# Phase changes of a fused transformer training kernel: PE transposes for two FFN groups, an earlier weight load, later tail loads

## Chip, cores and metric

One core of one Trainium2 chip. The time is device microseconds (us) of a whole execution. The kernel before took 3183.05 us in the median of its first three runs (3180.48 to 3196.14), all "fast" (within 1.5% of the fastest run of the same kernel). In the views PE is TensorE with its matmuls, DVE is VectorE, ACT ScalarE, POOL GpSimd, and SP (SPq: its queue) is SyncE, which here issues loads, DMA transposes and some stores. PE's results stand in banks of PSUM until DVE or ACT copies them out ("evacuation").

## The reference

A forward pass and its gradients. The reference is one `jax.vjp` over this function (2048 tokens, model width 448, 16 heads of 256, 8 memory rows, 64 segments of 32 tokens, FFN width 1792, all bf16):

```python
for s in range(n_seg):                       # recurrent: each segment needs the memory of the last
    xs = x[:, s*seg_len:(s+1)*seg_len, :]
    h = concatenate([mem, xs], axis=1)       # 8 + 32 rows
    q, k, v = h @ Wq, h @ Wk, h @ Wv         # 16 heads of 256
    p = softmax(where(mask, q k^T * scale, -1e9))
    o = (p v) @ Wo
    mem = o[:, :M, :]; outs.append(o[:, M:, :])
# ...
h  = x + A_ref(layernorm(x), mem0, Wq, Wk, Wv, Wo)
h2 = h + (silu(ln(h) @ w_gate) * (ln(h) @ w_up)) @ w_down
# outputs: h2 and the gradients of x, mem0, Wq, Wk, Wv, Wo, w_gate, w_up, w_down
```

## The kernel before

It has four phases: the forward chain over 64 segments; the FFN, forward and backward, in 8 groups of 256 tokens; the backward chain over the segments from 63 to 0; and the tail, which multiplies the weight gradients out of tensors that the other phases stored in DRAM. `W(o, ...)`, `A(o, ...)` and `B(o, ...)` are views at byte offset `o` (in KB per partition) of three fixed SBUF arenas. Different phases use the same bytes, and the dependence between two users of a byte becomes a wait. Names like X_q, M_v, DHb, VG or T0k are such tensors in DRAM. A scheduler orders each engine's instructions; `issue_after(x)` places an instruction behind `x` on the same engine.

The FFN's inputs are turned by PE for group 0 only, by DMA transposes on SP for the others; its products z, u and g are turned by DMA transposes and stored (in the last group u and g by PE):

```python
for n, gi in enumerate(groups):
    if n > 0:
        load_in(n, gi)                       # h and dout of the group, on SP
    for tt in range(G):
        # ... hn = (h - mean) * rstd  on DVE
        for src, dst in ((hn_t, hnT), (dout_t, doT)):
            if n == 0:
                # 4 PE transposes into PSUM, one evacuation
            else:
                nc.sync.dma_start_transpose(out=dst[:, :, tt*P:(tt+1)*P], in_=src)
    # ...
    proj(Wg_sb, hnT, gate)                   # ACT: sg = sigmoid(ps); DVE: g = ps * sg
    proj(Wu_sb, hnT, up)
    proj(WdT_sb, doT, dzf)
    # ... z, u, g -> Zt, DGP, DU:
    #     nc.sync.dma_start_transpose(out=stg, in_=...); nc.gpsimd.dma_start(out=dst, in_=stg)
```

The backward chain's weights go to the bytes that the FFN's weights leave; each segment writes its results to one of five buffers `blk_b`:

```python
blk_b = [A(8 * i, 32, P) for i in range(5)]
# ... loads on SP, in the program's order: segment 63's Q and K, To, v of 63, Tv, Tk, Tq
# (in the trace Tq stands ahead of Tk)
blk = {nm: blk_b[(3 * tb + i) % 5] for i, nm in enumerate("vkq")}
# ... in the last segment (s == 0), after its first products:
k.tl.grads(0)                                # tail loads of DHb, on SP
k.tl.outs(0, 3, 0, 6)                        # tail loads of X_o, on SP
```

The tail's first product reads those loads. Pieces of M_v are fetched by POOL into `ld_b = [A(33.5, ...), B(0, ...)]`, packed by DVE and ACT, and turned by PE for a later product.

Of the kernel before, what the change touches and what calls it, by code (L numbers as in the profile page):

```python
# [15 lines left out]
P = 128  # L16
# [249 lines left out]
class _FFNLoads:  # L266

    def __init__(self, k):
        W, D, F, KC, FC, G = k.W, k.D, k.F, k.KC, k.FC, 2
        self.k = k  # L270
        self.Wg_sb, self.Wu_sb = W(0, KC, F), W(14, KC, F)
        self.WdT_sb, self.Wd_sb = W(64, KC, F), W(78, FC, D)
        self.WgT_sb, self.WuT_sb = W(96, FC, D), W(108.25, FC, D)
        self.h_b = [W(32 + 0.875 * i, D) for i in range(4)]
        self.dout_b = [W(39.5 + i, k.DP) for i in range(4)]

# [18 lines left out]
    def at(self, place):  # L295
        k, sync = self.k, self.k.nc.sync
        if place == 0:
            self.rows(self.Wg_sb, k.aps["B_w_gate"])
            self.rows(self.Wu_sb, k.aps["B_w_up"])
        elif place == 1:  # L300
            self.load_in(0, 0)
        elif place == 2:
            self.turned_rows(self.WdT_sb, k.dr["Td"])
            sync.dma_start(out=self.Wd_sb, in_=k.aps["B_w_down"].rearrange("(c p) d -> p c d", p=P))
        else:
            sync.dma_start(out=self.WgT_sb, in_=k.dr["Tg"])
            return sync.dma_start(out=self.WuT_sb, in_=k.dr["Tu"])


class _TailLoads:  # L310

    def __init__(self, k):
        W, A, NT, NB = k.W, k.A, k.NT, k.NB
        self.k = k
        self.slots = [W(17.5 + 4 * i, 2048) for i in range(3)] + [A(25.5 + 4 * i, 2048) for i in range(2)] \
            + [A(48 + 4 * i, 2048) for i in range(3)] + [W(60, 2048), W(92, 2048)] + [W(96 + 4 * i, 2048) for i in range(7)] \
            + [W(32 + 4 * i, 2048) for i in range(7)] + [W(64 + 4 * i, 2048) for i in range(7)] + [A(17.5 + 4 * i, 2048) for i in range(2)]
        self.n = 0
        self.order = list(range(NT, NB)) + list(range(NT - 1, -1, -1))
        self.DCt = W(0, NB, k.D)  # L320
        self.x = {}

    def ring(self):
        self.n += 1
        return self.slots[(self.n - 1) % len(self.slots)]

    def grads(self, part):
        k, D, S, NT, M, SEG = self.k, self.k.D, self.k.S, self.k.NT, self.k.M, self.k.SEG
        sync, DHb = k.nc.sync, k.dr["DHb"]
        dcx = DHb[0:S, 0:D].rearrange("(t r i) d -> r i t d", r=4, i=SEG)  # L330
        dcm = DHb[S:, 0:D].rearrange("(t r m) d -> r m t d", r=4, m=M)
        dc8 = DHb[0:S, 0:D].rearrange("(g s i) d -> g s i d", s=16, i=SEG)
        if part == 0:
            for g in range(k.NB - NT):
                sync.dma_start(out=self.DCt[:, NT + g], in_=dc8[g, :, 0:M])
        for r in range(4):
            if part == 0:
                sync.dma_start(out=self.DCt[32 * r:32 * r + 24, :NT], in_=dcx[r, M:SEG])
                sync.dma_start(out=self.DCt[32 * r + 24:32 * r + 32, 4:NT], in_=dcm[r, :, 4:NT])
            else:  # L340
                sync.dma_start(out=self.DCt[32 * r + 24:32 * r + 32, 0:4], in_=dcm[r, :, 0:4])

    def outs(self, i0, i1, c0, c1):
        for t in self.order[i0:i1]:
            if t not in self.x:
                self.x[t] = self.ring()
            self.k.nc.sync.dma_start(out=self.x[t][:, c0 * P:c1 * P], in_=self.k.dr["X_o"][t][:, c0 * P:c1 * P])

# [438 lines left out]
def ffn_phase(k: _K, back):  # L787
# [14 lines left out]
    h_b, dout_b, load_in = fl.h_b, fl.dout_b, fl.load_in  # L802
    hn_b = [W(35.5 + i, DP) for i in range(4)]
    hnT_b = [W(28 + 2 * i, KC, G * P) for i in range(2)]
    doT_b = [W(43.5 + 2 * i, KC, G * P) for i in range(2)]
    t1 = W(47.5, G, FC, P)
    z_b = [A(56, G, FC, P), A(21, G, FC, P)]
# [24 lines left out]

    def tmajor_pe(src, t, tt, dst, i):
        stg = A(3.5 * i, F)
        for c0 in (0, 8):
            n = min(8, FC - c0)
            pt = k.ps1()[:].bitcast(BF16)
            for c in range(n):
                nc.tensor.transpose(pt[:, c * P:(c + 1) * P], src[:, tt, c0 + c, :], k.ident[:, :])
            k.evac(stg[:, c0 * P:(c0 + n) * P], pt[:, 0:n * P])  # L840
        nc.gpsimd.dma_start(out=dst[t * P:(t + 1) * P, :], in_=stg)

    def tmajor(src, t, tt, dst, z_last=False):
        stg = tstg_b[1 + tt] if z_last else tstg_b[rot[0] % 3]
        rot[0] += 1
        nc.sync.dma_start_transpose(out=stg, in_=src[:, tt].rearrange("p f n -> p (f n)"))
        nc.gpsimd.dma_start(out=dst[t * P:(t + 1) * P, :], in_=stg.rearrange("p f n -> p (f n)"))
# [19 lines left out]
    for n, gi in enumerate(list(range(last - 1)) + [last, last - 1]):  # L867
        hnT, doT = hnT_b[n % 2], doT_b[n % 2]
        if n > 0:
            load_in(n, gi)  # L870
        if n == last - 3:
            rstd(NT - 4, NT)
        if n == last:
            back()
        for tt in range(G):
# [7 lines left out]
            for src, dst in ((hn_t, hnT), (dout_t, doT)):  # L883
                if n == 0:
                    pt = k.ps1()[:].bitcast(BF16)
# [3 lines left out]
                else:  # L889
                    nc.sync.dma_start_transpose(out=dst[:, :, tt * P:(tt + 1) * P], in_=src)  # L890
            nc.gpsimd.dma_start(out=dr["HN"][rows, :], in_=hn_t[:, 0:D])
        e = n % 2
        g, z, dz, u, sg = g_b[e], z_b[e], dz_b[e], u_b[e], sg_b[e]
# [25 lines left out]
        for tt in range(G):  # L919
            t = G * gi + tt  # L920
            rows = slice(t * P, (t + 1) * P)
            tmajor(z, t, tt, dr["Zt"], n == last)
            pf = k.fx1()
# [3 lines left out]
            nc.vector.tensor_tensor(out=o_t, in0=pf[:, 0:D], in1=h_b[2 * e + tt], op=ALU.add)  # L927
            nc.gpsimd.dma_start(out=OUT0[rows, :], in_=o_t)
        for tt in range(G):
            nc.vector.tensor_tensor(out=u[:, tt], in0=dz[:, tt], in1=u[:, tt], op=ALU.mult)  # L930
            nc.vector.tensor_tensor(out=u[:, tt], in0=u[:, tt], in1=sg[:, tt], op=ALU.mult)
            nc.vector.tensor_tensor(out=g[:, tt], in0=dz[:, tt], in1=g[:, tt], op=ALU.mult)
        if n == last:
            back()
        for tt in range(G):
            t = G * gi + tt
# [17 lines left out]
        if n == last:  # L954
            for tt in range(G):
                t = G * gi + tt
                tmajor_pe(u, t, tt, dr["DGP"], 2 * tt)
                tmajor_pe(g, t, tt, dr["DU"], 2 * tt + 1)


def backward_chain(k: _K):
# [38 lines left out]
    def load_seg(s):  # L1000
        if s < NSEG - 1:
            load_v(s)
        for w, (nm, T_sb) in enumerate((("q", Q_sb), ("k", K_sb))):
            t1 = dr["T1"][s, :, w].rearrange("(g x i) n -> g i x n", g=2, x=2)
            t0 = dr["T0" + nm][s // 8].rearrange("(x s i) (g n) -> s g i x n", x=2, s=8, g=2)
            for g in range(2):
                for src, i0, i1 in ((t1[g], M, L), (t0[s % 8, g], 0, M)):
                    nc.sync.dma_start(out=T_sb[64 * g + i0:64 * g + i1].rearrange("p (x c) n -> p x (c n)", x=2), in_=src)
        P_sb = Pb[s % 2]
# [19 lines left out]
    prep_tile(NT - 1)  # L1029
    load_seg(NSEG - 1)  # L1030
    yield
    nc.sync.dma_start(out=WoT_sb[:, 0:3, :], in_=dr["To"][:, 0:3, :])
    nc.sync.dma_start(out=WoT_sb[0:64, 3, :], in_=dr["To"][0:64, 3, :])
    nc.gpsimd.memset(WoT_sb[64:P, 3, :], 0.0)
    yield
    v_in = load_v(NSEG - 1)
    with tc.issue_after(v_in.ins):
        nc.sync.dma_start(out=WvT_sb, in_=dr["Tv"])
    yield
    nc.sync.dma_start(out=WkT_sb, in_=dr["Tk"])  # L1040
    nc.sync.dma_start(out=WqT_sb, in_=dr["Tq"])
# [17 lines left out]
    for s in range(NSEG - 1, -1, -1):  # L1059
# [4 lines left out]
        lo = {nm: lo_b[nm][tb % len(lo_b[nm])] for nm in "kqv"}  # L1064
        blk = {nm: blk_b[(3 * tb + i) % 5] for i, nm in enumerate("vkq")}
        P_sb = Pb[s % 2]
# [5 lines left out]
        with k.prio.crit():  # L1072
# [26 lines left out]
            if s == 0:  # L1099
                k.tl.grads(0)  # L1100
                k.tl.outs(0, 3, 0, 6)
            pD3 = pD[:, 0:8 * L].rearrange("p (h n) -> p h n", n=L)
# [10 lines left out]
            def heads(nm, lhs, rhs):  # L1113
# [8 lines left out]
                if s == 0:  # L1122
                    k.tl.outs(*{"v": (3, 8), "k": (8, 9), "q": (9, 10)}[nm], 0, 6)

# [20 lines left out]
            rows_in("q", WqT_sb, 0, MC)  # L1145
            nc.vector.tensor_copy(out=om[:, 0:224], in_=pH[:, 0:224])
            nc.scalar.copy(out=om[:, 224:D], in_=pH[:, 224:D])
# [69 lines left out]
def tail_phase(k: _K):  # L1217
# [39 lines left out]
    def load_m(nm, hf):  # L1257
        todo = []
        for g in range(NG):
# [4 lines left out]
            def pack(ld=ld_b[g % 2], pk=pk_b[g % 2]):  # L1264
                nc.vector.tensor_copy(out=pk[:, 0:8], in_=ld[:, :, 0:8, :].rearrange("p s c m -> p c s m"))
                nc.scalar.copy(out=pk[:, 8:16], in_=ld[:, :, 8:16, :].rearrange("p s c m -> p c s m"))
# [9 lines left out]

    tl.outs(10, NB, 0, 6)
    tl.grads(1)
    tl.outs(0, NB, 6, 11)
    tl.outs(0, NB, 11, 16)  # L1280
    xo = tl.x
    nc.gpsimd.dma_start(out=HC, in_=dr["HC"].rearrange("(t p) d -> p t d", p=P)[:, :, 0:D])

# [39 lines left out]
    for hf in range(2):  # L1323
        xt = xo if hf == 0 else load_x("o", 1)
        j0 = 0
        for n in (6, 5, 5):
# [3 lines left out]
            rows_by_d(lambda b, i, j0=j0: xt[b][:, (j0 + i) * P:(j0 + i + 1) * P], lambda b: DCt[:, b, :], order, n, st)  # L1330
            j0 += n

    HN = W(0, NB, D)
# [99 lines left out]
```

## Time and profile before

| phase | from (us) | to (us) | length |
|---|---|---|---|
| forward chain | 0 | 1061.4 | 1061.4 |
| FFN, 8 groups | 1061.4 | 1409.0 | 347.6 |
| first backward segment (63) | 1409.0 | 1458.4 | 49.5 |
| segments 62 to 1 | 1458.4 | 2482.8 | 1024.3 |
| last segment (0), until the first tail matmul | 2482.8 | 2528.6 | 45.9 |
| tail | 2528.6 | 3198.7 | 670.1 |

These stretches come from PE's timeline: each begins with the first matmul of a known line (L855, L1079 of segments 63, 62 and 0, L1315). In a timeline a line has start, duration, engine, source line, operation, `out<-in`, form, count, and in brackets the idle time before it with what ended it. The prediction shows the lines of before.

### The profile page before, as it was taken

To read this page: it belongs to the slowest core of one execution; us is meant where nothing else is said; L and a number is where in the kernel's file an instruction comes from. 1 tells how busy PE (TensorE), PEld (TensorE's weight loads), DVE (VectorE), ACT (ScalarE), POOL (GpSimd) and SP (SyncE) were. 2 spreads that over 40 slices of the span, in tenths; PEclk is the share of its full clock that TensorE was granted. 3 is DMA by queue.
4 is the path that set the end of the run, shared out by engine and by line. 5 is a ranking of instruction groups with operands and counts; after the bars stand their busy time and mean duration, and the time that the engine had idled before them with its cause. 6 is when DMAs were issued, how large, how long until landed. Compare 5 with 4: busy or idle time off the path is not lost.

```text
span 3198.7 us, 107919 instructions
## 1 busy us (share of the span) xinstructions
PE 2917.2 (91%) x47442; PEld 1759.8 (55%) x47442; DVE 1367.3 (43%) x3433; ACT 1058.5 (33%) x2501; POOL 666.7 (21%) x1540
## 2 busy tenths in 40 slices
PE   6899999999998679968999999999999699999998
PEld 3555555555544456656666666666666454444443
DVE  4555455455455457654444544454444201111110
ACT  2444344344344233323333333333333101111110
POOL 2222222222222221121111211112111111111111
PEclk9999999999999889988999999999999899999999
DMA  6677666666756988894445555445445898969942
GB/s 235 169 170 176 172 168 176 172 170 167 196 156 164 280 194 194 197 309 107 126 138 137 143 138 140 126 131 155 132 138 145 262 266 223 199 181 194 197 142 66
DMA packets 763753, 556.21 MB, mean 174 GB/s; under 512 B 627732, under 2 KB 662404, under 8 KB 760852
## 3 DMA queue, kind: packets, MB, share of 16 engines
q1 hardware_dynamic: 708116, 373.96, 49.2%
q0 software_dynamic: 55168, 175.36, 16.3%
q8 instruction: 372, 6.09, 0.8%
q14 instruction: 97, 0.79, 0.1%
HBM read 167.32 MB, written 234.23 MB: 126 GB/s over the span
## 4 chain that ended last, share of the span: by engine, by line
PE 72%; DVE 9%; issue 8%; DMA 6%; ACT 3%; POOL 1%; SPq 1%; ACTq 0%; POOLq 0%; DVEq 0%
PE psf L1294 8%; PE po L1128 7%; PE psf L1079 6%; PE psf L526 5%; PE psf L637 5%; PE po L682 4%; PE psf L1056 4%; PE psf L1315 4%; PE fx L1192 3%; PE fx L945 2%; PE psf L855 2%; PE fx L455 2%; DVE arA L75 2%; PE psf L540 2%; PE fx L1299 2%
## 5 line engine op out<-in xcount | busy, mean ns | idle before, releaser
L75 DVE CAST arA<-psf 128x256 bf16<-128x256 f32 (+3 forms) x933 | 426.6, 479 | 826.1 <-PE psf L1294 258.9
L76 ACT CAST arA<-psf 128x96 bf16<-128x96 f32 (+5 forms) x915 | 352.4, 409 | 1084.7 <-PE psf L1294 256.5
L1128 PE MATMUL po<-arW,arA 128*32 128x448 bf16 x6144 | 351.2, 359 | 21.7 <-DVE arA L75 20.8
L1294 PE MATMUL psf<-arW,arA 128*128 128x512 bf16 x1000 | 252.0, 379 | 0.0
L1079 PEld LDWEIGHTS <-arW 128*128 128x128 bf16 x8192 | 213.9, 96 | 30.3 <-issue 30.3
L1079 PE MATMUL psf<-arA,arW 128*128 128x40 bf16 x8192 | 218.0, 180 | 11.1 <-issue 5.8
L1128 PEld LDWEIGHTS <-arA 128*32 128x32 bf16 x6144 | 152.7, 97 | 135.9 <-DVE arA L75 22.0
L1294 PEld LDWEIGHTS <-arA 128*128 128x128 bf16 x1440 | 135.9, 98 | 164.8 <-issue 13.7
L637 PE MATMUL psf<-arW,arA 128*64 128x512 bf16 x1536 | 219.7, 387 | 0.0
L855 PE MATMUL psf<-arW 128*128 128x256 bf16 x1344 | 155.4, 277 | 57.9 <-DMA arW<-arW 45.6
L526 PE MATMUL psf<-arW,arA 128*32 128x512 bf16 x3072 | 194.7, 386 | 12.5 <-DVE arA L724 12.5
L855 PEld LDWEIGHTS <-arW 128*128 128x128 bf16 x1344 | 133.1, 99 | 82.3 <-DMA arW<-arW 43.2
L76 ACT CAST arB<-psf 128x64 bf16<-128x64 f32 (+3 forms) x384 | 121.9, 318 | 146.1 <-PE psf L530 106.0
L682 PE MATMUL po<-arW,arA 128*32 128x256 bf16 (+1 forms) x4096 | 144.5, 267 | 10.8 <-DVE arA L75 7.5
L1056 PEld LDWEIGHTS <-arW 128*128 128x128 bf16 x2048 | 87.7, 100 | 90.4 <-issue 59.8
L1056 PE MATMUL psf<-arB,arW 128*128 128x80 bf16 x2048 | 98.2, 202 | 42.0 <-DMA arW<-T0k 23.1
L1089 ACT COPY arA<-psf 128x1024 bf16<-128x1024 bf16 x128 | 123.4, 1015 | 2.6 <-PE psf L1088 1.2
L526 PEld LDWEIGHTS <-arA 128*32 128x32 bf16 x3072 | 70.6, 97 | 90.8 <-DVE arA L724 18.1
L682 PEld LDWEIGHTS <-arA 128*32 128x32 bf16 x4096 | 95.8, 98 | 33.5 <-DVE arA L75 10.5
L455 PE MATMUL fx<-arA,arW 128*128 128x64 bf16 (+1 forms) x2048 | 84.2, 195 | 32.2 <-ACT arB L76 19.4
L76 ACT COPY arA<-psf 128x512 bf16<-128x512 bf16 (+2 forms) x136 | 79.0, 582 | 94.2 <-DVE arA L75 91.4
L455 PEld LDWEIGHTS <-arW 128*128 128x128 bf16 (+1 forms) x2048 | 70.6, 98 | 54.5 <-issue 32.7
(281 smaller groups left out, 4581.1 us busy)
## 6 DMA issues: line engine op xcount, KB each, us to landing
arW<-T SPq DMA_DIRECT2D x256, 128.0 KB
X_o<-arA SPq DMA_DIRECT2D x33, 512.0 KB
T<-arA SPq DMA_DIRECT2D x64, 256.0 KB
X_v<-arA POOLq DMA_DIRECT2D x32, 512.0 KB, 6.2
X_k<-arA POOLq DMA_DIRECT2D x32, 512.0 KB, 3.7
X_q<-arA POOLq DMA_DIRECT2D x32, 512.0 KB, 3.3
out_dram<-arA POOLq DMA_DIRECT2D x90, 128.0 KB, 4.0
VG<-arA SPq DMA_DIRECT2D x64, 160.0 KB
```

The costliest lines, as they stand in the source:

```text
L75: return nc.vector.tensor_copy(out=out, in_=in_)
L76: return nc.scalar.copy(out=out, in_=in_)
L455: nc.tensor.matmul(banks[w][:, i * 64:(i + 1) * 64], lhsT=lhsT, rhs=xr[lo:hi, kc, :], start=(kc == 0 and i == 0), stop=(kc == KC - 1), ski ...
L526: nc.tensor.matmul(banks[w][32 * q:32 * q + 32, :], lhsT=hT_roll[:, kc, sl, M:L], rhs=(Wq_sb, Wk_sb)[w][:, kc, col(q, b)], start=(kc == 0) ...
L637: nc.tensor.matmul(pV[b][64 * g:64 * g + 64, 0:512], lhsT=hT_flat[:, kc, sl * L:sl * L + 64], rhs=Wv_sb[:, kc, n * 512:(n + 1) * 512], sta ...
L682: nc.tensor.matmul(pO[32 * q:32 * q + 32, 0:w], lhsT=xblk[:, j, r * SEG:(r + 1) * SEG], rhs=Wo_sb[:, cj(j), 256 * dh:256 * dh + w], start= ...
L855: nc.tensor.matmul(ps[:, f2 * 256:(f2 + 1) * 256], lhsT=Wt[:, kc, c * P:(c + 1) * P], rhs=xT[:, kc, :], start=(kc == 0), stop=(kc == KC - 1))
L1056: nc.tensor.matmul(ps[b][:, i * 2 * L:(i + 1) * 2 * L], lhsT=lhs[:, at, :], rhs=rhs_bd[:, cl // 2, :, :].rearrange("p g n -> p (g n)"), st ...
L1079: nc.tensor.matmul(pss[b][:, jj * L:(jj + 1) * L], lhsT=WoT_sb[:, kc, c * P:(c + 1) * P], rhs=do_roll[:, kc, sl, :], start=(kc == 0), stop ...
L1128: nc.tensor.matmul(pH[32 * (j % 4):32 * (j % 4) + 32, 0:D], lhsT=blk[nm][:, j, r * SEG:(r + 1) * SEG], rhs=WT[:, cj(j), :], start=(nm == " ...
L1294: nc.tensor.matmul(pa[2 * kc + g][:, 0:w], lhsT=lhs_of(b)[:, kc * P:(kc + 1) * P], rhs=rhs_of(b, g), start=(b == 0), stop=(b == nblk - 1), ...
L1315: nc.tensor.matmul(pa[i][:, 0:D], lhsT=lhs_of(b, i), rhs=rhs_of(b), start=(bi == 0), stop=(bi == len(nblk) - 1))
```

## The change

The intent is to close the three gaps where phases meet: turn group 1 by PE too and load its inputs ahead; turn the last group's z by PE, load three quarters of Wk turned (Tk) during that group, and move `blk` by two buffers; let the last segment's K load go ahead of the tail loads. The core of the diff:

```diff
-        self.h_b = [W(32 + 0.875 * i, D) for i in range(4)]
-        self.dout_b = [W(39.5 + i, k.DP) for i in range(4)]
+        self.h_b = [W(o + 0.875 * i, D) for o in (37.75, 32) for i in range(2)]
+        self.hn_b = [W(o + i, k.DP) for o in (39.5, 33.75) for i in range(2)]
+        self.dout_b = [W(o + i, k.DP) for o in (41.5, 35.75) for i in range(2)]
@@ loads ahead of the FFN
             self.load_in(0, 0)
+            self.load_in(1, 1)
@@ FFN
-        if n > 0:
+        if n > 1:
             load_in(n, gi)
-                if n == 0:
+                if n < 2:
                     pt = k.ps1()[:].bitcast(BF16)     # PE transposes
@@ last group
-            tmajor(z, t, tt, dr["Zt"], n == last)
+            if n < last:
+                tmajor(z, t, tt, dr["Zt"])
@@ last group, after its products u and g
+                tmajor_pe(z, G * gi + tt, tt, dr["Zt"], (W(120.5, F), B(5, F))[tt])
@@ backward chain, weights
+    nc.sync.dma_start(out=WkT_sb[:, 8:MC], in_=dr["Tk"][:, 8:MC])
     yield
     # To ... Tv ... v of segment 63
-    nc.sync.dma_start(out=WkT_sb, in_=dr["Tk"])
+    nc.sync.dma_start(out=WkT_sb[:, 0:8], in_=dr["Tk"][:, 0:8])
     nc.sync.dma_start(out=WqT_sb, in_=dr["Tq"])
-        blk = {nm: blk_b[(3 * tb + i) % 5] for i, nm in enumerate("vkq")}
+        blk = {nm: blk_b[(3 * tb + i + 2) % 5] for i, nm in enumerate("vkq")}
@@ tail loads (all of grads(0) and outs)
+                with k.tc.issue_after(k.last_load.ins):
                     sync.dma_start(out=self.DCt[:, NT + g], in_=dc8[g, :, 0:M])
-                k.tl.outs(0, 3, 0, 6)
+                k.tl.outs(0, 7, 0, 6)
```

Cut: other slots for the tail's X_o tiles, the load of HC moved behind half of the first tail products, an `issue_after` for the first pack, and a `t1` and a `doT` buffer of their own for the last group.

More of the change, by code (lines that the diff above doesn't have):

```diff
@@ L314, in __init__ @@
         self.k = k
-        self.slots = [W(17.5 + 4 * i, 2048) for i in range(3)] + [A(25.5 + 4 * i, 2048) for i in range(2)] \
-            + [A(48 + 4 * i, 2048) for i in range(3)] + [W(60, 2048), W(92, 2048)] + [W(96 + 4 * i, 2048) for i in range(7)] \
-            + [W(32 + 4 * i, 2048) for i in range(7)] + [W(64 + 4 * i, 2048) for i in range(7)] + [A(17.5 + 4 * i, 2048) for i in range(2)]
+        self.first = [W(17.5 + 4 * i, 2048) for i in range(3)] + [A(4 * i, 2048) for i in range(4)]
+        self.slots = [A(48 + 4 * i, 2048) for i in range(3)] + [W(60, 2048), W(92, 2048)] + [W(96 + 4 * i, 2048) for i in range(7)] \
+            + [W(32 + 4 * i, 2048) for i in range(7)] + [W(64 + 4 * i, 2048) for i in range(7)] + [A(17.5 + 4 * i, 2048) for i in range(4)] + self.first[0:3]
         self.n = 0
@@ L323, in ring @@
     def ring(self):
+        if self.first:
+            return self.first.pop(0)
         self.n += 1
@@ L334, in grads @@
             for g in range(k.NB - NT):
-                sync.dma_start(out=self.DCt[:, NT + g], in_=dc8[g, :, 0:M])
+                with k.tc.issue_after(k.last_load.ins):
+                    sync.dma_start(out=self.DCt[:, NT + g], in_=dc8[g, :, 0:M])
         for r in range(4):
             if part == 0:
-                sync.dma_start(out=self.DCt[32 * r:32 * r + 24, :NT], in_=dcx[r, M:SEG])
-                sync.dma_start(out=self.DCt[32 * r + 24:32 * r + 32, 4:NT], in_=dcm[r, :, 4:NT])
+                with k.tc.issue_after(k.last_load.ins):
+                    sync.dma_start(out=self.DCt[32 * r:32 * r + 24, :NT], in_=dcx[r, M:SEG])
+                    sync.dma_start(out=self.DCt[32 * r + 24:32 * r + 32, 4:NT], in_=dcm[r, :, 4:NT])
             else:
@@ L346, in outs @@
                 self.x[t] = self.ring()
-            self.k.nc.sync.dma_start(out=self.x[t][:, c0 * P:c1 * P], in_=self.k.dr["X_o"][t][:, c0 * P:c1 * P])
+            with self.k.tc.issue_after(self.k.last_load.ins):
+                self.k.nc.sync.dma_start(out=self.x[t][:, c0 * P:c1 * P], in_=self.k.dr["X_o"][t][:, c0 * P:c1 * P])
 def forward_chain(k: _K):
@@ L802, in ffn_phase @@
     h_b, dout_b, load_in = fl.h_b, fl.dout_b, fl.load_in
-    hn_b = [W(35.5 + i, DP) for i in range(4)]
+    hn_b = fl.hn_b
     hnT_b = [W(28 + 2 * i, KC, G * P) for i in range(2)]
     doT_b = [W(43.5 + 2 * i, KC, G * P) for i in range(2)]
-    t1 = W(47.5, G, FC, P)
+    t1_b = [W(47.5, G, FC, P), A(14, G, FC, P)]
+    doT_last = A(0, KC, G * P)
     z_b = [A(56, G, FC, P), A(21, G, FC, P)]
@@ L831, in ffn_phase, with tmajor_pe @@
     rot = [0]
-    def tmajor_pe(src, t, tt, dst, i):
-        stg = A(3.5 * i, F)
+    def tmajor_pe(src, t, tt, dst, stg):
         for c0 in (0, 8):
@@ L841, in tmajor_pe, with tmajor @@
         nc.gpsimd.dma_start(out=dst[t * P:(t + 1) * P, :], in_=stg)
-    def tmajor(src, t, tt, dst, z_last=False):
-        stg = tstg_b[1 + tt] if z_last else tstg_b[rot[0] % 3]
+    def tmajor(src, t, tt, dst):
+        stg = tstg_b[rot[0] % 3]
         rot[0] += 1
@@ L867, in ffn_phase @@
     for n, gi in enumerate(list(range(last - 1)) + [last, last - 1]):
-        hnT, doT = hnT_b[n % 2], doT_b[n % 2]
-        if n > 0:
+        hnT, doT = hnT_b[n % 2], doT_b[n % 2] if n < last else doT_last
+        t1 = t1_b[n == last]
+        if n > 1:
             load_in(n, gi)
@@ L872, in ffn_phase @@
             rstd(NT - 4, NT)
-        if n == last:
-            back()
         for tt in range(G):
@@ L891, in ffn_phase @@
             nc.gpsimd.dma_start(out=dr["HN"][rows, :], in_=hn_t[:, 0:D])
+        if n == last:
+            back()
         e = n % 2
@@ L928, in ffn_phase @@
             nc.gpsimd.dma_start(out=OUT0[rows, :], in_=o_t)
+        if n == last:
+            back()
         for tt in range(G):
@@ L934, in ffn_phase @@
             back()
+            for tt in range(G):
+                tmajor_pe(z, G * gi + tt, tt, dr["Zt"], (W(120.5, F), B(5, F))[tt])
         for tt in range(G):
@@ L956, in ffn_phase @@
                 t = G * gi + tt
-                tmajor_pe(u, t, tt, dr["DGP"], 2 * tt)
-                tmajor_pe(g, t, tt, dr["DU"], 2 * tt + 1)
+                tmajor_pe(u, t, tt, dr["DGP"], A(7 * tt, F))
+                tmajor_pe(g, t, tt, dr["DU"], A(7 * tt + 3.5, F))
 def backward_chain(k: _K):
@@ L1007, in load_seg @@
                 for src, i0, i1 in ((t1[g], M, L), (t0[s % 8, g], 0, M)):
-                    nc.sync.dma_start(out=T_sb[64 * g + i0:64 * g + i1].rearrange("p (x c) n -> p x (c n)", x=2), in_=src)
+                    k.last_load = nc.sync.dma_start(out=T_sb[64 * g + i0:64 * g + i1].rearrange("p (x c) n -> p x (c n)", x=2), in_=src)
         P_sb = Pb[s % 2]
@@ L1035, in backward_chain @@
     yield
-    v_in = load_v(NSEG - 1)
-    with tc.issue_after(v_in.ins):
-        nc.sync.dma_start(out=WvT_sb, in_=dr["Tv"])
+    nc.sync.dma_start(out=WvT_sb, in_=dr["Tv"])
     yield
-    nc.sync.dma_start(out=WkT_sb, in_=dr["Tk"])
+    load_v(NSEG - 1)
+    yield
+    nc.sync.dma_start(out=WkT_sb[:, 0:8], in_=dr["Tk"][:, 0:8])
     nc.sync.dma_start(out=WqT_sb, in_=dr["Tq"])
@@ L1122, in heads @@
                 if s == 0:
-                    k.tl.outs(*{"v": (3, 8), "k": (8, 9), "q": (9, 10)}[nm], 0, 6)
+                    k.tl.outs(*{"v": (7, 10), "k": (10, 11), "q": (11, 12)}[nm], 0, 6)
             def rows_in(nm, WT, j0, j1):
@@ L1145, in backward_chain @@
             rows_in("q", WqT_sb, 0, MC)
-            nc.vector.tensor_copy(out=om[:, 0:224], in_=pH[:, 0:224])
+            k.last_om = nc.vector.tensor_copy(out=om[:, 0:224], in_=pH[:, 0:224])
             nc.scalar.copy(out=om[:, 224:D], in_=pH[:, 224:D])
@@ L1264, in pack @@
             def pack(ld=ld_b[g % 2], pk=pk_b[g % 2]):
-                nc.vector.tensor_copy(out=pk[:, 0:8], in_=ld[:, :, 0:8, :].rearrange("p s c m -> p c s m"))
+                with tc.issue_after(k.last_om.ins):
+                    nc.vector.tensor_copy(out=pk[:, 0:8], in_=ld[:, :, 0:8, :].rearrange("p s c m -> p c s m"))
                 nc.scalar.copy(out=pk[:, 8:16], in_=ld[:, :, 8:16, :].rearrange("p s c m -> p c s m"))
@@ L1275, in load_m @@
         return todo
-    tl.outs(10, NB, 0, 6)
+    tl.outs(12, NB, 0, 6)
     tl.grads(1)
@@ L1281, in tail_phase @@
     xo = tl.x
-    nc.gpsimd.dma_start(out=HC, in_=dr["HC"].rearrange("(t p) d -> p t d", p=P)[:, :, 0:D])
     def d_by_e(lhs_of, rhs_of, nblk, widths, store, at=None):
@@ L1331, in tail_phase @@
             j0 += n
+        if hf == 0:
+            nc.gpsimd.dma_start(out=HC, in_=dr["HC"].rearrange("(t p) d -> p t d", p=P)[:, :, 0:D])
     HN = W(0, NB, D)
```

## The prediction

> **What bounds the kernel now.** I read the page first, then the PE waits, then the chain of waits around each phase boundary, last the timelines of the queues that feed PE there.
>
> The page says that PE is busy for 91% of the span, and its row of 40 slices (80 us each) falls to 6 or 7 around 1040 to 1200, 1360 to 1440 and 2480 to 2560, where phases change (the first slice is the start).
>
> ```profile
> PE 2917.2 (91%) x47442; PEld 1759.8 (55%) x47442; DVE 1367.3 (43%) x3433; ACT 1058.5 (33%) x2501; POOL 666.7 (21%) x1540
> PE   6899999999998679968999999999999699999998
> ```
>
> So time can only be won where PE stands idle. The view of PE's waits between 1040 and 2560 us (engine, line, what it waited for, total, times, longest) holds few long ones:
>
> ```profile
> PE psf L855 <- DMA arW<-arW: 45.6, 4, 35.0
> PE psf L1056 <- DMA arW<-T0k: 23.1, 1, 23.1
> PE po L1128 <- DVE arA L75: 20.8, 1, 20.8
> PE psf L1056 <- ACT arB L76: 4.5, 1, 4.5
> ```
>
> 35.0 + 20.8 + 4.5 + 23.1 = 83.4 us sit in three places. PE's timeline dates them:
>
> ```profile
> 1133.14 12.52 PE L855 MATMUL psf<-arW 128*128 128x256 bf16 x96 [35.00 <-DMA arW<-arW]
> ...
> 1439.72 1.31 PE L1128 MATMUL po<-arW,arA 128*32 128x448 bf16 x12 [20.81 <-DVE arA L75]
> 1450.76 1.23 PE L1056 MATMUL psf<-arB,arW 128*128 128x80 bf16 x16 [4.54 <-ACT arB L76]
> ...
> 2516.90 1.22 PE L1056 MATMUL psf<-arB,arW 128*128 128x80 bf16 x16 [23.14 <-DMA arW<-T0k]
> ```
>
> Gap 1: FFN group 1 waits for its four DMA transposes of h and dout. They come last in SP's order:
>
> ```profile
> 1103.72 3.41 SPq L547 DMA_TRANSPOSE arA<-arA  x1
> 1107.49 3.26 SPq L846 DMA_TRANSPOSE arB<-arA  x1
> 1110.85 6.20 SPq L547 DMA_TRANSPOSE arA<-arA  x1
> 1117.14 4.24 SPq L846 DMA_TRANSPOSE arW<-arA  x2
> 1121.48 4.08 SPq L890 DMA_TRANSPOSE arW<-arW  x1
> ```
>
> Gap 2: the first backward segment runs from 1408.97 to 1458.43, 49.5 us; a steady one takes 16.0 (1642.19 to 1658.23). DVE stands 21.05 us behind the store of DGP, and that store behind POOL, which stands behind the store of DHb:
>
> ```profile
> 1439.11 0.56 DVE L75 CAST arA<-psf 128x384 bf16<-128x384 f32 x1 [21.05 <-DMA DGP<-arA]
> ...
> 1427.34 0.20 POOL L1044 MEMSET arB<- 128x128 f32 x1 [20.59 <-DMA DHb<-arB]
> ...
> 1443.36 0.52 POOL L1046 MEMSET omb<- 128x512 f32 x1 [12.64 <-DMA DH<-dh_t]
> ```
>
> DMA is full here: share 0.99 and 418 GB/s from 1409 to 1440, with three weight loads of 3584 KB. Gap 3: in the last segment the load of K (T0k) is issued at 2512.84, after 20 us of tail loads of DHb and X_o.
>
> **What the Trainium skill says.** "DMA: Bandwidth & Descriptors", section "Issuing engines are not separate DMA queues": transfers started by scalar, sync or gpsimd run on the same 16 engines and interleave. The trace agrees: a 128 KB store issued at 1406.2 held POOL until 1427.3 while the weights loaded. The same page, "Anatomy of one DMA — SWDGE (gpsimd) path", gives a fit of 2.0 us plus bytes over 436 GB/s, and says that waits are taken by the issuing sequencer before dispatch. The fit makes 3.2 us of 512 KB; around gap 3 such stores of X_v took 9.5, so under load I use the trace. The second point is what gaps 1 and 3 show: a load stands behind its queue's earlier entries. "TensorE: Matmul & The Clock Gate", Part 1: after an idle window of about 3.4 us PE falls to 4/8 clock and needs as long to come back. The trace agrees: granted clock 0.50 from 2500 to 2520; 96 matmuls of L855 took 12.52 us after gap 1 and 10.64 in group 2. So each closed gap may give 2 us more.
>
> **Gap 1, part by part.** h and dout of groups 0 and 1 are loaded ahead, and group 1 is turned by 16 more PE transposes (16 took 1.06 us at 1059.82) with 4 evacuations. Four DMA transposes and two loads leave SP. hnT of group 1 is then ready at about 1105, so the 35 us wait goes. But from the instruction order of the changed kernel, group 1's first sigmoid results and L897 write buffers whose bytes still hold the last forward transposes (L547) and the last store of X_o. That store was issued at 1120.22 and lands about 6 us later, 1126; the SP entries ahead of it hardly change, as one more L846 comes forward and two loads go. PE can fill its free PSUM banks and then waits. I put the L897s at 1127 in place of 1138: 11 us gained (8 to 16). The later groups keep their DMA transposes; waits of 7.29, 1.96 and 1.37 us before groups 4 to 6 move to other groups, plus or minus 4.
>
> **Gap 2, part by part.** Removed: the DGP wait (blk buffers rotate by two, out of the staging's bytes), two DMA transposes of z, and 2.75 of 3.67 MB of Tk from the crowded stretch. Added: 28 PE transposes of z; 54 of that kind took 3.18 us, so 28 x 59 ns = 1.65 us, on PE's path. Left: POOL's memset L1044 still follows the store of DHb, memset L1046 the store of DH, and all k rows follow the last 0.92 MB of Tk, which SP issues after L263. Three loads of 3.67 MB ran from 1408 to 1437.5 at about 9.6 us each; with Tv earlier and Tk cut to a quarter, Tq and Tk end at about 1428 to 1434. The next segment starts at 1437 to 1440 rather than 1458.43: 18 to 21 gained, less 1.65, and 1 back from the clock: 18 us (12 to 25).
>
> **Gap 3, part by part.** Every tail load is now held behind the last K load. This removes the wait of 23.1 us, and segment 0 could be finished at 2504. But the first tail matmul (L1315) started at 2528.61 with no wait at all, 11.7 us after the gap; two things can now hold it. The tail loads start 3 us later; from the first load's issue at 2486 their landing took until 2511 (2491.09 + 19.88), so now 2513. And the changed order puts 8 PE transposes of the packed M_v piece in front of that first tail matmul; before, they came some 1200 PE instructions later. They need a load of M_v whose buffer now overlaps the blk buffers that X_q is stored from, so it waits for both X_q stores (512 KB, 6.4 us each) behind X_v (9.5), M_v (10.3) and X_k (10.5) on the same POOL queue: X_v, X_k and X_q twice 0.52 MB each, M_v, M_k and M_q 0.26 each, so 3.9 MB of stores and a 0.5 MB load from 2489 on. At 119 to 150 GB/s (an estimate: that queue moved 5.23 MB from 2486 to 2530, 119 GB/s, and may do more when the others rest) 4.4 MB end at 2519 to 2526. L1315 then starts at about 2524, not 2528.6: 4 us gained (0 to 15). The bulk of the 23 us becomes a new wait. The tail itself is matmul after matmul from 2528 to 3191 and keeps its time; moving the HC load by half a product saves nothing, since PE did not wait for it.
>
> **Sum.** 11 + 18 + 4 = 33 us of 3183: 3150 us.
>
> **The rivals.** (a) The gaps close as intended: 83.4 us less 3 of added PE work, plus some 6 of clock, gives about 3097, 2.7% faster. For it: all four waits named are removed by name. Against: in each gap the trace shows a second thing that ends within 20 us of the first (X_o at 1126, DHb, DH and weights at 1422 to 1437, M_v). (b) A transfer takes the place of the removed wait everywhere and the bytes are the bound: DMA is full in all three stretches (share 1.12, 0.99, 1.00), and nearly all bytes remain. Gap 1 then yields 8, gap 2 12, gap 3 0: 3163. For it: the shares. Against: in gap 2 at least 2.75 MB leave the stretch, and at 1440 to 1459 the DMA share is only 0.49, so those last 19 us were latency. (c) The added PE work and shifted transposes cost later groups more than I say: 4 us up. A slower kernel would need a new wait of over 60 us net, for which I see no source.
>
> **Range and chances.** I believe the middle: 3150. The low end, 3120, takes 16 + 25 + 15 + 6 of clock (62); the high end, 3166, takes 8 + 12 + 0 and 3 lost in groups. The threshold of 2% is 3119.4, about the low end, and (a) lies past it: 0.2 for faster, 0.79 for the same, 0.01 for slower.
>
> **What would show it.** Gap 1: PE starts L855 of group 1 near 1105 instead of 1133, stops after a few banks, and its next wait names DVE L897 or ACT, with an X_o store behind it; if group 1 runs through, (a) holds there. Gap 2: no DVE wait on DGP; k rows (L1128) wait for Tk or for POOL's L1044; the next segment starts near 1438 less the shift of gap 1. Gap 3: no wait for T0k; a new PE wait of 15 to 20 us just before the first L1315, on DVE L1265, ACT L1266 or loads of X_o. Without it I am wrong by that amount. A span of the tail (first L1315 to end) other than 662 us would also break the argument.

## The result

The changed kernel took 3149.2 us in the median of four runs (3144.86 to 3154.7) against 3181.77 for before. The ratio is 0.9889 (95% interval 0.9855 to 0.9922): 1.1% faster, within the 2% that count as the same. A ratio here compares the fast runs of two kernels in the same rounds, so it is not quite the ratio of the medians. Repeated in another set of runs it was 0.9887 (0.9861 to 0.9912).

The page of the changed kernel (busy times; then PE's busy tenths in 40 slices):

```profile
PE 2909.6 (92%) x47476; PEld 1759.7 (56%) x47486; DVE 1369.8 (43%) x3437; ACT 1061.9 (34%) x2505; POOL 670.1 (21%) x1540
PE   5899999999988879989999999999999799999998
```

Counted from the left, the 14th and 18th slices have risen from 6 to 8, the 19th from 8 to 9, the 32nd from 6 to 7; the 1st and 12th fell by one. (A slice is a fortieth of the span, so the 14th starts at 1040 us before and at 1024 us here.) PE's waits between 1040 and 2560 us (engine, line, what it waited for, total, times, longest; line numbers are 7 to 14 higher than before):

```profile
PE ph L1287 <- DVE lnb_m1s L257: 14.3, 1, 14.3
PE psf L862 <- DVE arA L905: 13.0, 1, 13.0
PE psf L862 <- DMA arW<-arW: 12.1, 4, 5.6
...
PE psf L862 <- DVE lnb_m2s L259: 8.6, 1, 8.6
...
PE po L1142 <- DMA arW<-Tk: 7.5, 1, 7.5
PE psf L1111 <- DMA arA<-VG: 6.3, 1, 6.3
```

The waits of 35.0, 20.8 and 23.1 us are gone, and of the 45.6 us for DMA transposes 12.1 are left, in four pieces. But in each place a new wait stands. 14.3 + 13.0 + 8.6 + 7.5 + 6.3 = 49.7 us of new waits replace 83.4. The 8.6 us stand ahead of group 1's first matmul. DVE's timeline shows the cause, which the view of waits doesn't name:

```profile
1101.30 0.40 DVE L887 TENSOR_SCALAR arW<-arW,mv,rstd 128x448 bf16<-128x448 bf16 x1 [9.14 <-DMA arW<-Hh]
```

L887 is the normalisation of group 2. DVE waits there for that group's h, and so makes its copy of group 1's turned inputs only at 1102.74; group 1's first matmul starts at 1103.22. What is behind the 13.0 and the 14.3 is in the chain of waits (start, duration, what), first between group 0 and group 1, then in the last segment:

```profile
1112.58 4.96 DMA arA<-arA
1117.57 0.47 issue
1118.06 4.09 DMA X_o<-arA
...
1122.23 0.70 DVE arA L905
```

```profile
2457.11 12.32 DMA X_q<-arA
...
2470.06 9.46 DMA arA<-M_v
...
2479.64 0.43 DVE arA L1280
2480.07 0.07 DVE lnb_m1s L257
2480.14 1.02 PE ph L1287 x8
```

Group 1's first DVE product waits for the store of X_o, the forward chain's last work. The first tail matmul stands behind eight PE transposes (L1287), these behind the packed M_v piece (L1280; the view names the DVE instruction just after it), that behind the M_v load, and that behind the stores of X_q whose bytes it takes.

| stretch (us) | before | before, 2nd trace | changed | changed, 2nd trace |
|---|---|---|---|---|
| forward chain | 1061.4 | 1057.8 | 1056.2 | 1058.3 |
| FFN | 347.6 | 343.5 | 337.5 | 336.2 |
| first backward segment | 49.5 | 50.4 | 34.1 | 34.3 |
| segments 62 to 1 | 1024.3 | 1015.1 | 1015.1 | 1019.2 |
| last segment | 45.9 | 45.3 | 38.1 | 37.8 |
| tail | 670.1 | 670.4 | 668.7 | 670.7 |
| span | 3198.7 | 3182.4 | 3149.6 | 3156.6 |

The two traces first at hand differ by 49.1 us, half as much again as the medians of the runs do. The first trace of before came from a long execution (3200.6 us): its forward chain and its steady segments, which the change does not touch, were 5 and 9 us longer than in the other. Only the stretches tell that apart, and a second trace settles it.

### The profile page after: what moved, and what is told of

It is laid out like the page before. It is cut to its first block, busy times and chain, and to the rows that moved or that the text cites. A ratio compares the mean times of both kernels' runs of the same rounds, so it can differ in the third digit from the quotient of the medians.

```text
span 3149.6 us, 107994 instructions
## 1 busy us (share of the span) xinstructions
PE 2909.6 (92%) x47476; PEld 1759.7 (56%) x47486; DVE 1369.8 (43%) x3437; ACT 1061.9 (34%) x2505; POOL 670.1 (21%) x1540
## 4 chain that ended last, share of the span: by engine, by line
PE 74%; DVE 9%; issue 7%; DMA 5%; ACT 3%; POOL 1%; SPq 1%; ACTq 0%; POOLq 0%; DVEq 0%
PE psf L1308 8%; PE po L1142 7%; PE psf L1093 7%; PE psf L533 5%; PE psf L644 5%; PE po L689 4%; PE psf L1070 4%; PE psf L1329 4%; PE fx L1206 3%; PE fx L958 3%; PE fx L462 2%; DVE arA L75 2%; PE psf L862 2%; PE psf L547 2%; PE fx L1313 2%
## 5 line engine op out<-in xcount | busy, mean ns | idle before, releaser
L1308 PE MATMUL psf<-arW,arA 128*128 128x512 bf16 x960 | 241.9, 379 | 0.0
L1093 PEld LDWEIGHTS <-arW 128*128 128x128 bf16 x8192 | 214.2, 96 | 26.3 <-issue 26.3
L462 PE MATMUL fx<-arA,arW 128*128 128x64 bf16 (+1 forms) x2048 | 83.4, 194 | 32.7 <-ACT arB L76 19.3
L689 PEld LDWEIGHTS <-arA 128*32 128x32 bf16 x4096 | 95.7, 98 | 31.8 <-DVE arA L75 10.8
```

The lines of the kernel that those rows point to most:

```text
L462: nc.tensor.matmul(banks[w][:, i * 64:(i + 1) * 64], lhsT=lhsT, rhs=xr[lo:hi, kc, :], start=(kc == 0 and i == 0), stop=(kc == KC - 1), ski ...
L689: nc.tensor.matmul(pO[32 * q:32 * q + 32, 0:w], lhsT=xblk[:, j, r * SEG:(r + 1) * SEG], rhs=Wo_sb[:, cj(j), 256 * dh:256 * dh + w], start= ...
L1093: nc.tensor.matmul(pss[b][:, jj * L:(jj + 1) * L], lhsT=WoT_sb[:, kc, c * P:(c + 1) * P], rhs=do_roll[:, kc, sl, :], start=(kc == 0), stop ...
L1308: nc.tensor.matmul(pa[2 * kc + g][:, 0:w], lhsT=lhs_of(b)[:, kc * P:(kc + 1) * P], rhs=rhs_of(b, g), start=(b == 0), stop=(b == nblk - 1), ...
```

## The experiments

All twelve gave correct results. Times of single experiments scatter too much to tell 3 us (the eleven runs of before on one chip went from 3182 to 3203), so the verdicts rest on stretches, of one trace for each experiment, and on how far these scatter where nothing was edited.

### The kernel before once more

No edit.

> The unchanged kernel once more, for a second trace. The trace shown of before belongs to its longest run (3196.1 us against a median near 3182), while the trace of the changed kernel belongs to a typical one. By the traces the changed kernel starts the FFN 5.2 us earlier and crosses 62 steady backward segments 9.2 us faster, though neither stretch was changed on purpose. Theory: that is scatter of the first trace, so this second trace starts the FFN near 1056 and takes about 1015 us for those segments, with a time of 3180 to 3184. Rival: the change did speed up those stretches, and this trace repeats 1061 and 1024.

Measured: FFN start at 1057.8, steady segments 1015.1 us, time 3184.43 (a single run, so of unknown state; its clock of 0.974 is that of fast runs). The gaps repeat: waits of 35.2, 22.8 and 22.8 us. So the 14 us were scatter of the first trace, and the theory holds. In all fourteen traces the forward chain takes 1052 to 1064 us and the steady segments 1013 to 1025.

### Group 1 by PE alone

```diff
             self.load_in(0, 0)
+            self.load_in(1, 1)
-        if n > 0:
+        if n > 1:
             load_in(n, gi)
-                if n == 0:
+                if n < 2:
```

> Kernel before with only FFN group 1 turned by the PE and loaded ahead. Theory: group 1 then stands behind the last X_o store of the forward chain, 11 us gained (8 to 16), ratio 0.9965 (0.995 to 0.9975); PE's wait of 35 us becomes one of about 13 on DVE plus one of about 9 ahead of it. Rival 1: the whole 35 us come back, ratio 0.989. Rival 2: the later groups give the gain back because the same DMA transposes come later, ratio 0.9995.

Measured: ratio 0.9985 (0.9957 to 1.0013), too coarse to decide. The FFN took 337.3 us, and PE's timeline shows the predicted pair of waits:

```profile
1103.88 6.73 PE L856 MATMUL psf<-arW 128*128 128x256 bf16 x40 [8.57 <-DVE lnb_m2s L259]
1124.03 9.50 PE L856 MATMUL psf<-arW 128*128 128x256 bf16 x64 [13.42 <-DVE arA L898]
```

PE starts group 1 at 1103.9, does 40 matmuls (five PSUM banks of eight) and stops until 1124.0. In the four traces without this part the FFN took 343.5 to 347.6 us (mean 345.1), in the eight with it and no further edit of the FFN 333.1 to 337.5 (mean 335.5): 9.6 us gained. Neither rival holds.

### The changed kernel without that part

The same edit taken back.

> Changed kernel with group 1 turned by DMA again. Theory: the three parts add up, so what is left is 0.9889 less the gain of the first part: about 23 us gained, ratio 0.9925 (0.991 to 0.994), and the 35 us wait of PE before group 1 is back. Rival: the parts depend on each other (transfers of one stage shift the next), and this one with the first part alone misses the whole by over 6 us.

Measured: ratio 0.9929 (0.9903 to 0.9955); FFN 345.7, first segment 31.1, last segment plus tail 708.9, and the wait before group 1 is back with 31.4 us. 0.9929 x 0.9985 = 0.9914 against 0.9889: taken as they stand, the ratios miss the whole by 8 us, more than the rival's 6, but each has an interval of 8 to 9 us to either side and can't decide. By stretches the parts add up: 7.8 us in the FFN of the first part alone, 18.5 and 7.6 here, together 33.9. The theory holds by the stretches alone.

### The K load first, alone

```diff
+                    k.last_load = nc.sync.dma_start(out=T_sb[64 * g + i0:...], in_=src)
@@ every tail load
+                with k.tc.issue_after(k.last_load.ins):
```

> Kernel before with only the tail loads held behind the last K load; buffers, slots and the turn of the blk buffers as before, so the M_v piece does not wait for the stores of X_q and its transposes stand late in PE's order. Theory: the 23.1 us wait goes; the first tail matmul is then held only by tail loads of DHb and X_o, which land some 20 us after issue: it starts 5 to 15 us earlier than before, ratio 0.996 (0.9945 to 0.998). Rival 1: the bytes are the bound and PE waits for X_o or DHb loads until the old time, ratio 0.9995. Rival 2: all 23 us come back, ratio 0.9925.

Measured: ratio 0.9987 (0.9962 to 1.0013), outside the theory's range; the interval takes in rival 1 too. The wait for T0k is gone, and the last segment takes 37.6 us instead of 45.6, 8 us less as the theory had it, but last segment plus tail only 710.1 against 716.5 (mean of three traces without the edit): 6.4 us of 23. The expectation that the M_v transposes would stand late in PE's order was wrong; they moved ahead here too. PE's timeline:

```profile
2495.55 0.29 PE L1275 MATMUL ph<-ident,arA 128*128 128x128 bf16 x1 [8.84 <-DVE arA L1268]
...
2504.07 2.05 PE L1318 MATMUL psf<-arW 128*128 128x448 bf16 x5 [4.94 <-DMA arW<-X_o]
```

Here `blk` keeps its old bytes, the M_v piece is ready at 2495.5, and PE still waits for X_o until 2504.1. So the tail loads are a bound of their own, which ends about as late (37.6 us after the segment's start) as the M_v piece in the changed kernel (37.3).

### Group 1 in its own buffers

```diff
         g, z, dz, u, sg = g_b[e], z_b[e], dz_b[e], u_b[e], sg_b[e]
+        if n == 1:
+            g, z, dz, u, sg = A(21,...), A(49,...), A(56,...), W(54.5,...), A(0,...)
```

> Changed kernel, with the five intermediate buffers of FFN group 1 placed in bytes that the forward chain's last transposes and stores do not hold (those which group 0 has done with). Nothing else changes. Theory: PE's wait of 13.0 us on the DVE product of group 1, behind the last X_o store, goes, and group 1 runs through from 1103: the FFN stage takes 325 us instead of 337.5 (322 to 330), ratio to before 0.985 (0.983 to 0.987). Rival: group 2's inputs, which SP turns behind the same forward work, become the next wait and eat most of it: FFN stage 333 to 337, ratio 0.988 to 0.9895.

Measured: ratio 0.9888 (0.9862 to 0.9913), FFN 334.4 us, inside the spread of unedited kernels (333.1 to 337.5). The rival holds. The wait itself did go; PE's timeline of groups 1 and 2:

```profile
1099.38 12.64 PE L862 MATMUL psf<-arW 128*128 128x256 bf16 x96 [8.90 <-DVE lnb_m2s L259]
...
1152.45 9.01 PE L862 MATMUL psf<-arW 128*128 128x256 bf16 x56 [7.77 <-DVE arA L907]
```

Group 1 now runs its 96 matmuls without a stop, 13 us are won, and group 2 loses 7.8 of them. The DVE and SP timelines show why:

```profile
1149.52 0.42 DVE L887 TENSOR_SCALAR arW<-arW,mv,rstd 128x448 bf16<-128x448 bf16 x1 [11.07 <-DMA arW<-Hh]
```

```profile
1129.41 16.61 SPq L853 DMA_TRANSPOSE arW<-arA  x3
1146.07 1.24 SPq L283 DMA_DIRECT2D arW<-Hh  x1
```

DVE works in order. Ahead of group 2's products it has the normalisation of group 3 (L887), whose h is loaded by SP (L283), behind three DMA transposes of group 1's outputs. Of the 16.6 us SP spent 5.8 on these. The rest it waited, before the third, until the store of Zt had left the staging buffer which that one writes (SP's waits from 1125 to 1165 us):

```profile
SPq L853 <- DMA Zt<-arW: 10.6, 1, 10.6
```

What PE no longer waits for in one group, SP's order makes it wait for in the next; other waits for DMA transposes (up to 7.9 us) follow. A further staging buffer was not tried.

### Tk ahead of Tq

```diff
-    nc.sync.dma_start(out=WkT_sb[:, 0:8], in_=dr["Tk"][:, 0:8])
-    nc.sync.dma_start(out=WqT_sb, in_=dr["Tq"])
+    tk8 = nc.sync.dma_start(out=WkT_sb[:, 0:8], in_=dr["Tk"][:, 0:8])
+    with tc.issue_after(tk8.ins):
+        nc.sync.dma_start(out=WqT_sb, in_=dr["Tq"])
```

> Changed kernel, with the last quarter of Tk issued ahead of Tq. Theory: the bytes bound the first backward segment, so the wait of 7.5 us for Tk shrinks but the q rows then wait for Tq: the first segment takes 31 us instead of 34.0 (29.5 to 33), ratio 0.988. Rival: only the order of the two loads holds PE; then all 7.5 us come back and the segment takes 26.5.

Measured: ratio 0.989, first segment 31.5 us. The wait moved from k rows to q rows, as the theory said (PE's timeline, first of the changed kernel, then of this one):

```profile
1419.58 6.00 PE L1142 MATMUL po<-arW,arA 128*32 128x448 bf16 x64 [7.45 <-DMA arW<-Tk]
```

```profile
1427.01 3.06 PE L1143 MATMUL po<-arW,arA 128*32 128x448 bf16 x32 [6.75 <-DMA arW<-Tq]
```

The rival (26.5 us) is out. But seven traces with this stretch as the change left it have 31.1 to 34.9 us (mean 33.4), so 31.5 is no proven gain.

### The DGP and DU stores held as well

```diff
+            k.held.append(lambda: nc.gpsimd.dma_start(out=dst[t * P:(t + 1) * P, :], in_=stg))
@@ at the end of the next segment
+                later(s - 1, "start", fn)
```

> Changed kernel with Tk's last quarter ahead of Tq, and with the four stores of DGP and DU of the last group (1.84 MB) held until the second backward segment. Theory: the bytes bound the first segment, so 1.84 MB less at about 370 GB/s take 5 us more off: 26.5 us (25 to 29) against 31.5 with the swap alone and 34.0 without. Rival: what bounds it is the moment at which the weight loads are issued, or POOL's memset behind the store of DH; then it stays at 30 us or more.

Measured: ratio 0.9878 (0.9853 to 0.9904), first segment 33.0 us: the theory of the bytes falls. The stores were indeed out of the stretch (POOL issued them at 1429.96 and later), yet Tq came no earlier. SP's and PE's timelines:

```profile
1393.45 9.84 SPq L1015 DMA_TRANSPOSE arA<-VG  x1
...
1407.53 0.32 SPq L1060 DMA_DIRECT2D arW<-Tq  x1
```

```profile
1423.41 3.18 PE L1147 MATMUL po<-arW,arA 128*32 128x448 bf16 x32 [4.57 <-DMA arW<-Tq]
```

From the segment's first matmul (1396.32) to the last weight's landing it is 27.1 us; with the stores in place it was 26.3 (swap alone) and 25.9 (changed kernel). Tq was issued 11.2 us into the segment, with the swap alone 9.3, and its first use came 15.9 us after that against 17.0: so 1.84 MB less were worth about 1 us of its transfer, not 5. Tq goes out so late because SP has first spent 9.8 us on the transpose of VG behind the load of Tv. That fits the rival, the moment of issue; a kernel with Tq ahead of that transpose was not run, so it stays open.

### The M_v transposes later

```diff
                     for i in range(8):
-                        nc.tensor.transpose(pt[...], pk[...], ident[:, :])
+                        with tc.issue_after(k.first_pass.ins):      # last matmul of the X_o products
+                            nc.tensor.transpose(pt[...], pk[...], ident[:, :])
```

> Changed kernel, with the 16 transposes of the packed M_v piece held behind the first product of the tail. Theory after the trace of the K load alone: the X_o and DHb loads are a second bound that ends only some 3 us before the M_v piece does; the stretch from the last segment's start to the first tail matmul goes from 38.1 to 35.5 us (34 to 37), PE then waits 10 to 12 us for X_o or DHb, ratio 0.988. Rival: the M_v piece alone holds PE, then the stretch takes 24 us and the ratio is 0.9845.

Measured: ratio 0.9891 (0.9866 to 0.9916). The last segment takes 33.3 us instead of 38.1, but the tail 673.8: together 707.1, against 706.8 to 709.3 (mean 708.5) in six traces without an edit here. PE's timeline shows what took over:

```profile
2473.68 2.05 PE L1330 MATMUL psf<-arW 128*128 128x448 bf16 x5 [10.30 <-DMA arW<-X_o]
...
2497.24 1.11 PE L1330 MATMUL psf<-arW 128*128 128x448 bf16 x5 [2.95 <-DMA arW<-X_o]
```

10.30 + 2.95 = 13.25 us for X_o in place of 14.30 for M_v. The theory of a second bound holds; the stretch shrank a little more than expected, and the first product gave it back.

### The first tiles first as well

```diff
                     sync.dma_start(out=self.DCt[:, NT + g], in_=dc8[g, :, 0:M])
+            self.outs(0, 4, 0, 6)            # ahead of the other loads of DHb
-                k.tl.outs(0, 7, 0, 6)
+                k.tl.outs(4, 7, 0, 6)
```

> The kernel with the later turn, and the X_o loads of the four tiles that the tail multiplies first put ahead of the 1.7 MB of DHb loads of the other tiles. Theory: the order of landing counts, not the sum of bytes: the stretch shrinks to 31 us (28 to 34), ratio 0.9865, and later matmuls of the first tail product wait 1 to 4 us. Rival: the bytes bound it, the tail starts earlier but waits in its first product for as long, so the time equals that of the kernel with the later turn alone within 2 us.

Measured: ratio 0.989 (0.9871 to 0.9909). The last segment takes only 21.3 us, beyond what the theory said, and the tail 683.8: together 705.1. The rival holds, to within 2 us of the kernel with the later turn alone. The waits stand inside the first product, one of them longer than the 1 to 4 us of the theory:

```profile
2485.41 2.04 PE L1331 MATMUL psf<-arW,arA 128*128 128x448 bf16 x5 [7.42 <-DMA arA<-X_o]
...
2503.65 2.03 PE L1331 MATMUL psf<-arW 128*128 128x448 bf16 x5 [2.23 <-DMA arW<-DHb]
```

### The X_v and X_k stores held as well

```diff
+                if s == 0 and fn in (due[0][0], due[1][0], due[5][0], due[6][0]):
+                    k.held_tail.append(fn)   # issued behind the first product's stores
```

> Changed kernel with the later turn, the first four X_o tiles first, and the stores of X_v and X_k of the last tile (2.1 MB) held behind the first tail product. Theory: the bytes between the last segment and the end of the first tail product bound this change of phase, so last segment plus tail take 700 us (698 to 703) against 705.1 with those stores in place[...]. Rival: the order or the issue of the loads bounds it, and the sum stays at 705 to 707.

Measured: ratio 0.9886 (0.9861 to 0.9911), last segment plus tail 709.5 us, no gain. It does not decide between the theories, because the scheduler put ACT's half of the pack ahead of an older copy, and the M_v wait came back that way (timelines of ACT and PE):

```profile
2484.53 1.04 ACT L1285 COPY arA<-arA 128x1024 bf16<-128x1024 bf16 x1 [20.08 <-DMA arA<-M_v]
2485.48 0.53 ACT L1213 COPY om<-fx 128x448 f32<-128x448 f32 x1
```

```profile
2486.05 1.84 PE L1217 MATMUL fx<-sel,om 128*128 128x32 f32 x8 [15.83 <-ACT om L1213]
```

With 2.1 MB of stores out of the way the M_v piece still landed 36 us after the segment's start (2448.6), as late as in the changed kernel (36.8).

### The changed kernel once more

No edit.

> The changed kernel once more, as the base for the three that follow. Theory: 33 us faster than before, ratio 0.989 to 0.9905, with the stretches of its first trace to within 4 us (FFN 337.5, first segment 34.0, steady segments 1015 to 1025, last segment plus tail 706.8). Rival: the first figure was a lucky set of executions, and the ratio comes out over 0.992.

Measured: ratio 0.9887 (0.9861 to 0.9912), median 3154.19; its stretches are in the table above, all within the spread. The theory holds.

### All edits together

> All the edits that helped a stage in one kernel: group 1 in its own buffers, with the normalisation of group 3 queued on DVE behind group 2's gates; Tk first with DGP and DU stores held; later turn, first tiles first, X_v and X_k stores held. Theory: the stretches add up: FFN 331 us (328 to 334.5), first segment 26.5, last segment plus tail 700, so 15 to 20 us faster than the changed kernel, ratio to before 0.984 (0.9815 to 0.987). Rival: the gains of the FFN are again given back in later groups and bytes held now collide later; then 0.987 to 0.989.

Measured: ratio 0.9902 (0.9877 to 0.9926), median 3157.52, on the same chip and in the same rounds as the repeat of the changed kernel (3154.19). Its trace has FFN 332.5, first segment 33.0, last segment plus tail 708.9, so only the FFN could have gained. The rival's part holds that gains are given back, and the time even missed its range. The tail doesn't test the theory any more than in the run before: PE waited 15.5 us for the same copy on ACT (L1223 here). The further edit of this kernel, which puts DVE's normalisation of group 3 behind group 2's gates, was not run alone. None of these edits makes a kernel that beats the changed one.

## Why the prediction was right

**The sum.** Predicted 11 + 18 + 4 = 33 us. By the means of the stretches, over all traces that have a part against all that don't, it was 9.6 (345.1 to 335.5) + 16.2 (49.6 to 33.4) + 8.0 (716.5 to 708.5) = 33.8, and the medians differ by 32.6. So the total hides no large errors, but smaller ones that cancel: gap 3 was taken 4 us too small, gaps 1 and 2 1.4 and 1.8 too large. That the sum came within 1 us is in part luck.

**Gap 1.** The step that carried it, that group 1's first products find their bytes still held by the last X_o store, is shown: PE started at 1103.22 (1105 predicted), did five banks' worth, and waited 12.97 us more for DVE behind that store. From the start of the FFN to DVE's first L905 of group 1 it was 66.1 us, against 76.8 (1138.19 - 1061.36) before: 10.8 gained. The experiment with own buffers adds what the prediction did not see, a third wait behind it in SP's order.

**Gap 2.** The DGP wait went and the k rows waited for the last of Tk. The 28 transposes cost 1.73 us of PE (1.65 predicted). Not foreseen was the wait of 6.30 us for the transpose of segment 63's VG: the change put the load of Tv ahead of it, and SP spent 9.51 us on it, 1.37 before. POOL's memsets, named as what would be left, did not hold PE. That bytes set the moment, as rival (b) had it, is not shown: 1.84 MB fewer did not shorten the segment. This gap's edits were never run one by one, so how the 16.2 us divide among the turn of z, the early Tk and the move of `blk` stays open.

**Gap 3.** The new wait was 14.30 us (15 to 20 predicted) on the pack named. Its chain was sized roughly right in sum, not in its parts: the first tail matmul came 38.1 us after the segment's start, 41.2 predicted, but the X_q stores landed after 12.3 us, not 6.4, and M_v's load took 9.5. The gain was 8.0 rather than 4, inside the 0 to 15 that the prediction allowed. It named the second bound as well, the tail loads, but dated it too early, 30 us after the segment's start (2513): PE waited for X_o until 33.3 us with M_v out of its way, and until 37.6 with the K load first alone. So the two bounds give nearly the same time. (Its "1200 PE instructions" are not in the trace: before, the M_v transposes start 684 matmuls after the first L1315.)

**The tail.** 662 us were meant to PE's last matmul; so counted it is 663.0 before and 661.5 after, and to the end of the span 670.1 and 668.7. It kept its time, as assumed.

**The clock.** The 2 us that each closed gap "may give" did not come at gap 1, where two waits stand in place of one: group 1's first 104 matmuls took 6.79 + 9.75 = 16.54 us at granted clocks of 0.66 and 0.73, some 5 us more than at the rate of group 2 (100 in 11.08, clock 1.00). Before, the loss was 12.52 - 10.64 = 1.9. At gap 2, the Trainium skill's "TensorE: Matmul & The Clock Gate", Part 1, which has PE at 4/8 clock after an idle window of about 3.4 us, fits: the 64 row matmuls after the 7.45 us wait took 6.00 us at a granted clock of 0.53, where 64 of the same kind take 2.26 + 1.31 = 3.57 us in segment 0.

**Rival (a),** 83.4 us back, failed for the reason given against it: behind each wait stood another within 20 us.

## What to carry to other kernels

Before adding up the waits that a change removes, ask of each what else PE, or the engine that frees PE's PSUM, needs at that moment and when it comes: the gain is the distance to that second wait, and here it was 34 of 83 us. Where loads, stores and transposes of two phases share queues and bytes, closing a gap further hands it on: own buffers, another load order or a later transpose moved 7 to 13 us of wait to the next group, the next rows or into the next product. Compare stretches of several traces, not two totals, when the effect is 1% and executions of one kernel lie up to 0.65% apart.

## What the Trainium skill lacked or had wrong

- "DMA: Bandwidth & Descriptors", section "Anatomy of one DMA — SWDGE (gpsimd) path": its fit (2.0 us plus bytes over 436 GB/s) gives an estimate of 3.2 us for 512 KB, and the fit itself has no term for other traffic. Here, with a DMA share (mean busy share of the 16 DMA engines) of 0.94 from 2446 to 2480, the last X_q store took 12.3 us in the chain and a 512 KB load of M_v 9.5. The measurement decides; here the fit is a lower end.
- The same page, section "DMA Transpose (X-bar)": it gives constraints but not how long the issuing sequencer spends on one while loads are under way (cycle counts elsewhere on the page leave out the transfer). SP spent 1.37 us on the transpose of segment 63's VG before, ahead of the load of Tv, and 9.51 after, behind it; on segment 62's, behind further weight loads, 22.88 and 12.36; on segment 61's 1.33 after. What stood behind one in SP's order went out only then.
- None of the pages read speaks of the scatter of equal work inside one execution: most of the 62 equal backward segments take 15.6 to 17.3 us, but in 13 of the 14 traces one or a few take 17.4 to 21.0, up to some 10 us per execution. They differ from trace to trace, yet some recur: segment 32 in five traces, 44 in four. The cause stays open.
